# A fused linear-attention and MLP kernel: the first tile of x loaded in two halves on two queues, and the head's loads and steps in a new order

## The chip, the cores and the metric

The kernel runs on one NeuronCore of a Trainium2 chip. The metric is device time in microseconds, from the median of several executions. Instructions run on TensorE (PE; its weight loads are listed as PEld), VectorE (DVE), ScalarE (ACT), GpSimd (POOL) and SyncE (SP, which here only issues transfers). ScalarE issues some transfers too. In the profile a queue's issue of a transfer stands as SPq or ACTq.

## The reference

With S = 2048 tokens, width D = 640, 32 heads of 20 and a hidden width of 1728, it computes, in bf16:

```python
xn = layernorm(x)                              # over the last axis
qkv = (xn @ wqkv).reshape(B, S, 3, 32, 20).transpose(2, 0, 3, 1, 4)
q, k, v = qkv[0], qkv[1], qkv[2]
phi = lambda t: where(t > 0, t + 1, exp(t)) + 1e-6
kv  = einsum("bhsd,bhse->bhde", phi(k), v)
z   = einsum("bhsd->bhd", phi(k))
num = einsum("bhqd,bhde->bhqe", phi(q), kv)
den = einsum("bhqd,bhd->bhq", phi(q), z)[..., None] + 1e-6
s   = (num / den).transpose(0, 2, 1, 3).reshape(B, S, D) @ wo
g   = silu(relu(xn @ w1) @ w2)
out = x + s * g
```

## The kernel before, in words

The tokens are 16 tiles of 128 rows, tile t being x rows 128 t to 128 t + 127. The kernel's body records operations (engine, what is read, what is written) with a small scheduler, and the scheduler then works out every wait. The order in which operations are recorded is a text, PROGRAM (line 346), of short words that a player (line 1572) looks up. Up to the bar "|" the text is the head: there every engine keeps the text's order. Behind the bar TensorE and SP still keep it, while VectorE, ScalarE and GpSimd take, of the steps that are ready, those that are due first by the planner's costs (lines 44 to 83 for compute, 147 to 166 for transfers; lags, line 205, are two delays that the planner adds to the transfer line once it has passed a given time).

The words that matter here:

- lxN loads tile N of x (160 KB) on SP's queue, line 562; axN does so on ScalarE's queue. lkAB loads rows 128 A to 128 B of the key weight, 160 KB for each 128 rows, line 586. lwN loads a block of w1 (320 KB), line 582.
- baN and bbN take VectorE's statistics over the first and the second half of tile N (line 637), agN combines them (line 641). For tiles 0 and 3 the mean of the first half comes from VectorE (mhN, line 679) and of the second half from ScalarE (maN, line 685); for tiles 1 and 2 ScalarE sums the whole row. ceN subtracts the mean (lines 695 and 699; for tile 0 in two parts).
- trN transposes the centred tile with five TensorE products against an identity (line 706), cdN and caN copy the result to SBUF on VectorE or ScalarE (lines 716 and 718). kTAB multiplies tile T with key weight rows A to B (line 733); each such row block is two products of 320 columns. In the head only tiles 0 to 3 go this way.
- sqN squares a centred tile on ScalarE for its variance. SN and NN are statistics and norm of the other tiles (lines 637 to 673); each norm is followed by a DMA transpose on SP (line 722). Tiles 0 to 7 are transposed so in the head, in the order 1, 4, 5, 7, 6, 0, 2, 3.
- keN and krN are the exponential and the relu of the key product (line 743), FN their sum (lines 759 and 761). PN is a block of relu(x w1) over the first four tiles (line 823, with lw blocks 2 and 5 for P4, P5, P10 and P11). KTN is the key product of a later tile, from the DMA transposes (line 733).
- pfN and the products at the start (fill, line 604) are idle products: TensorE multiplies constants, 128 columns for each unit of the count, in products of up to 512 columns. The result is never read.

Behind the bar come Strassen-like units of seven products (line 1164 for 512-column ones, line 991 for 320-column ones) with operand sums on VectorE (line 936); the first such unit over tiles 0 to 7 needs all eight DMA transposes. The rest of the program, some 170 us, is made of such units and their evacuation, and the output of the last tiles.

The order around the change, in the head before, is this on each queue. SP: x0, x2, key weight 0 to 2, x3, key weight 2 to 4, x4, x5, key weight 4 to 5, x7, w1 block 2, x6, w1 blocks 5, 3 and 0, then the eight DMA transposes. ScalarE: x1, then the means of tiles 0, 1 and 2. VectorE: first half of tile 0's statistics, half mean, centring of tiles 0 and 1, first copy, second half of the statistics, centring of tile 2, two more copies. TensorE: 32 units of idle products, transposition of tile 0, three units of idle products, transposition of tile 1, key products of tile 0, transposition of tile 2, and so on.

Of the kernel before, what the change touches and what calls it, by code (L numbers as in the profile page):

```python
# [4 lines left out]
ALU = mybir.AluOpType  # L5
# [90 lines left out]
class Sched:  # L96
# [43 lines left out]

    def _record(self, E, kind, fns, R, W, extra, sem=None):
        o = _Op()
        o.E, o.kind, o.fns, o.n = E, kind, fns, len(self.recs)
        o.sem, o.need = sem if isinstance(sem, tuple) else (sem, 16)
        o.deps = set(self._hazards(R, W)) | set(extra)
        o.byt = 0
        if kind == "dma":
            seen = _Seen()
            fns[0](seen)
            name, a, _k = seen.call  # L150
            o.turn = "transpose" in name
# [35 lines left out]
    def place(self):  # L187
# [7 lines left out]
        t = sum(o.occ for o in queue["PE"]) + 10.0  # L195
# [15 lines left out]
        while left:  # L211
# [23 lines left out]
            est, E, c = best  # L235
# [115 lines left out]
SH0_1 F2 lx8 lq SH0_2 F3 lw6 wb KT7 KT6 xb wa SQ S8 xa n8 H110 n12 F6 H14 a0.s1 rb n11 F7  # L351
SM F4 SH0_3 xc T0 SH0_4 n13 H15 SK a0.s5 a0.s6 a0.s2 n9 H111 a0.s7 p1.s1 a0.s3 p1.s5 a0.s4 SH1 p1.s6 n10 n14 n15
y0 p1.s2 m0.s1 m0.s5 p1.s3 m0.s6 p1.s7 m0.s2 y4 y3 m0.s7 p1.s4 m0.s3 Kb8 m0.s4 a1.s5 a1.s1 F5 y2 Ka12 p0.s1 y1 p0.s5 a1.s6
a1.s2 p0.s6 a1.s7 a1.s3 y7 Ka8 a1.s4 p0.s2 a2.s5 a2.s1 y8 p0.s3 p0.s7 a2.s6 y5 y6 hh0 Ka11 T1 a2.s7 p0.s4 a2.s2 a2.s4 a2.s3
# [3 lines left out]
b2.s4 m1.s1 GT1 b2.s3 GT2 m1.s5 b3.s1 m1.s6 m1.s2 b3.s5 b3.s6 m1.s7 m1.s3 b3.s2 ZS b3.s7 b3.s3 m1.s4 c1 b5.s1 b3.s4 b5.s5 b4.s5 b5.s6  # L358
b4.s1 b5.s2 b5.s7 sl b4.s6 b5.s3 zc w2b b5.s4 b4.s7 b4.s3 g0.s1 g0.s5 b4.s4 g0.s6 b4.s2 GT3 w2c dn hh1 w2d GT4 wo g0.s3
GS1 g1.s1 do0 g1.s5 g0.s2 g1.s6 g0.s7 rc0 g1.s7 do1 g1.s2 dv0 g1.s3 g1.s4 wv1 uSa0 uT1 g0.s4 uT3 wv0 uT2 uSb0 u0.s1 u0.s5  # L360
kv1 do2 kv0 rc1 W5 u0.s6 uT4 W4 u0.s2 W1 u0.s7 uSa1 W3 u0.s3 uSa2 uSb2 W0 u1.s1 u0.s4 W2 uSb1 u1.s5 u1.s6 u2.s5
u2.s1 u1.s2 u1.s7 oT u2.s6 u1.s3 u1.s4 oS0 u2.s2 xre o0.s1 u2.s7 uSa4 o0.s5 o0.s6 u2.s3 do3 u2.s4 o0.s7 o0.s2 oS1 o0.s3 uSa3 u4.s1
# [8 lines left out]
def bass_recurrent_scan__linear_attn_block__dense_activation_relu__prompt_kernel(  # L371
# [14 lines left out]
    P = 128  # L386
# [6 lines left out]
    HN = D // 2  # L393
# [5 lines left out]
    x2 = A_x[0]  # L399
# [45 lines left out]
    xin = reg7[:, :].rearrange("p (t n) -> p t n", t=XR)  # L445
# [4 lines left out]
    def eks(t):  # L450
        return t % 4 if t < 8 else t % 3
# [33 lines left out]
    F0 = 6 * D  # L485
# [71 lines left out]
    def xs(t):  # L557
        return t if t < XR else (t - 4) % XR

    def x_load(t, n=1, E="SP", extra=()):  # L560
        sl = xs(t)
        dma(E, lambda eng: eng.dma_start(xin[:, sl:sl + n, :],
                                         x2[P * t:P * (t + n), :].rearrange("(t p) n -> p t n", p=P)),
            W=[("xin", sl + i) for i in range(n)], extra=extra)
# [39 lines left out]
    def fill(n):  # L604
        sc.group("PE", [(lambda eng, w=w: eng.matmul(ps[7][:, 0:w], lhsT=wide[:, 0:P], rhs=wide[:, 0:w], start=True, stop=True))
                        for w in [4 * P] * (n // 4) + [P * (n % 4)] * (n % 4 > 0)], W=[("ps", 7)])
# [28 lines left out]
    def bn(t, a):  # L635
        xv = xin[:, xs(t), :]
        sc.op("DVE", lambda eng: eng.bn_stats(stats[:, t, a, :], xv[:, HN * a:HN * (a + 1)]),  # L637
              R=[("xin", xs(t))], W=[("stats", t, a)])
# [44 lines left out]
    def mean_act(t, lo):  # L683
        junk = ek[:, eks(t), 0, 0:D - lo]
        sc.op("ACT", lambda eng: eng.activation(out=junk, in_=xin[:, xs(t), lo:D], func=ACTF.Copy, scale=1.0 / D,
                                                accum_out=msum[:, t, 1:2]),
              R=[("xin", xs(t))], W=[("msum", t, 1), ("ek_e", eks(t))])
        sc.allow_unread.add(("ek_e", eks(t)))

    def centre(t):  # L690
        split = ((0, P * TS), (P * TS, D)) if t == 0 else ((0, D),)
        for part, (c0, c1) in enumerate(split):
            key = ("xn", t, 0) if t == 0 and part == 0 else ("xn", t)
            if t in (1, 2):
                sc.op("DVE", lambda eng, c0=c0, c1=c1: eng.tensor_scalar(
                    out=xn[:, t, c0:c1], in0=xin[:, t, c0:c1], scalar1=msum[:, t, 1:2], scalar2=None,
                    op0=ALU.subtract), R=[("xin", t), ("msum", t, 1)], W=[key])
            else:
                sc.op("DVE", lambda eng, c0=c0, c1=c1: eng.tensor_scalar(
                    out=xn[:, t, c0:c1], in0=xin[:, t, c0:c1], scalar1=msum[:, t, 0:1], scalar2=msum[:, t, 1:2],  # L700
                    op0=ALU.subtract, op1=ALU.subtract), R=[("xin", t), ("msum", t, 0), ("msum", t, 1)], W=[key])
# [1280 lines left out]
```

## Time and profile before

| what | value |
|---|---|
| runs, device time | 202.53, 202.60 and 204.0 us; median 202.60 |
| the profiled execution | 202.56 us |
| its span, first to last instruction | 201.3 us |
| TensorE busy | 197.2 us, 98% of the span |
| VectorE, ScalarE, GpSimd busy | 173.2, 132.5, 37.7 us |
| transfers | 30.43 MB, 151 GB/s on the mean |

The span is shorter than the execution by what lies around the first and the last instruction. A row of the timeline has start, length, engine, line, operation, what is written and read, and at its end how long the engine stood idle before it and what released it. The rows of the chain of waits have start, length and what held the program's end in that stretch. TensorE's products are pipelined and their ends are modelled, so two products in a row overlap by the latency; the distance of two starts is the true cost of one.

### The profile page before, as it was taken

Reading aid. Unit: us, or ns where it says so; the run is one execution under the profiler, and the core shown is the slowest. Engines: PE = TensorE matmul, PEld = TensorE weight load, DVE = VectorE, ACT = ScalarE, POOL = GpSimd, SP = SyncE. Lnnn points to the kernel's source line nnn. Section 1 sums busy time; section 2 is a strip of 40 time slices with the busy share of each in tenths; the row PEclk is TensorE's granted clock in tenths of the full one; section 3 lists DMA queues with packets and bytes.
Section 4 is the critical chain, followed back from the end, with each engine's and each line's share of the span. In section 5 each row is a group of like instructions: output and inputs, shape, how many; then the busy total and the mean of one; then the engine's idle time right before and its main releaser. Section 6 shows DMA issues by size and latency. Waiting matters only on the chain.

```text
span 201.3 us, 3641 instructions
## 1 busy us (share of the span) xinstructions
PE 197.2 (98%) x1312; PEld 120.1 (60%) x1312; DVE 173.2 (86%) x407; ACT 132.5 (66%) x280; POOL 37.7 (19%) x66
## 2 busy tenths in 40 slices
PE   8899999999999999999999999999999999999995
PEld 2656534554564554545454777777777777777773
DVE  5998799999999989999568998999867699866565
ACT  6798958998999998868832514363545355536533
POOL 3584003143345646422000000000000000000000
PEclk9999999999999999999999999999999999999999
DMA  5999695345466798854304985975952711011113
GB/s 179 335 259 95 150 351 144 70 98 109 108 145 134 150 256 174 171 99 67 113 17 118 270 264 184 295 212 148 355 185 72 258 65 36 33 67 65 36 65 98
DMA packets 38455, 30.43 MB, mean 151 GB/s; under 512 B 13733, under 2 KB 38437, under 8 KB 38437
## 3 DMA queue, kind: packets, MB, share of 16 engines
q1 hardware_dynamic: 32853, 23.62, 41.8%
q0 software_dynamic: 4624, 5.57, 14.3%
q10 hardware_dynamic: 960, 1.02, 1.7%
q8 instruction: 10, 0.16, 0.4%
q14 instruction: 8, 0.07, 0.1%
HBM read 15.81 MB, written 5.24 MB: 105 GB/s over the span
## 4 chain that ended last, share of the span: by engine, by line
PE 90%; DVE 4%; DMA 2%; ACT 1%; issue 1%; DVEq 0%
PE psT L991 43%; PE psT L1164 32%; PE psT L733 6%; PE psT L1494 2%; PE psT L823 2%; DMA reg<-reg 1%; ACT regE L743 1%; PE psT L1838 1%; DMA reg<-in_A_x_dram 1%; PE psT L841 1%; PE psT L1629 1%; PE psT L1603 1%; DVE stats L637 1%; DVE regX L936 1%; PE psT L895 1%
## 5 line engine op out<-in xcount | busy, mean ns | idle before, releaser
L1164 PE MATMUL psT<-reg 128*128 128x512 bf16 (+2 forms) x166 | 45.0, 370 | 0.0
L991 PE MATMUL psT<-reg,regH 128*128 128x320 bf16 (+1 forms) x224 | 35.0, 299 | 0.0
L991 PE MATMUL psT<-reg 128*128 128x320 bf16 (+1 forms) x178 | 28.4, 299 | 0.0
L991 PEld LDWEIGHTS psT<-reg,regH 128*128 128x128 bf16 (+1 forms) x224 | 21.9, 98 | 8.5
L1164 PEld LDWEIGHTS psT<-reg 128*128 128x128 bf16 (+1 forms) x166 | 15.9, 98 | 16.9 <-DVE regH L1217 0.6
L863 POOL DMA_DIRECT2D regH<-reg x16 | 18.6, 1188 | 20.9 <-DMA regH<-reg 9.4
L991 PEld LDWEIGHTS psT<-reg 128*128 128x128 f16 (+1 forms) x178 | 17.3, 98 | 7.4 <-DVE regE L899 0.4
L936 DVE TENSOR_TENSOR reg<-reg 128x1024 f16<-128x1024 bf16 (+11 forms) x30 | 19.0, 646 | 2.2 <-PE psT L991 1.8
L998 ACT ACTIVATE reg<-psT 128x320 f32<-128x320 f32 (+1 forms) x24 | 10.5, 436 | 15.8 <-PE psT L991 14.8
L1214 ACT ACTIVATE regH<-psT 128x512 bf16<-128x512 f32 (+1 forms) x24 | 14.6, 612 | 5.8 <-PE psT L1164 5.3
L1665 ACT ACTIVATE wv_sb<-psT 128x320 bf16<-128x320 f32 (+2 forms) x23 | 9.6, 424 | 11.4 <-PE psT L991 11.0
L991 PE MATMUL psT<-reg,pqT 128*128 128x320 bf16 (+1 forms) x84 | 15.8, 299 | 0.0
L936 DVE TENSOR_TENSOR psT<-psT,reg 128x320 f32<-128x320 f32 (+1 forms) x21 | 11.4, 543 | 2.8 <-PE psT L991 2.8
L637 DVE BATCH_NORM_STATS2 stats<-reg 128x6 f32<-128x320 bf16 x28 | 12.3, 480 | 1.4 <-DMA reg<-in_A_x_dram 1.1
L1853 ACT ACTIVATE reg<-psT 128x640 bf16<-128x640 f32 (+1 forms) x14 | 8.0, 570 | 7.5 <-PE psT L991 7.5
L733 PE MATMUL psT<-reg 128*128 128x320 bf16 x80 | 12.3, 299 | 0.0
L936 DVE TENSOR_TENSOR reg<-psT,reg 128x320 bf16<-128x320 f32 (+1 forms) x16 | 7.8, 489 | 5.1 <-PE psT L991 5.1
L1171 ACT ACTIVATE psT<-psT 128x512 f32<-128x512 f32 (+1 forms) x18 | 10.6, 594 | 1.8 <-PE psT L1164 1.7
L800 ACT ACTIVATE regE<-psT 128x512 bf16<-128x512 f32 x16 | 9.5, 603 | 2.6 <-PE psT L1164 2.5
L998 ACT ACTIVATE psT<-psT 128x320 f32<-128x320 f32 x17 | 7.2, 425 | 5.6 <-PE psT L991 5.5
L936 DVE TENSOR_TENSOR reg<-reg,wv_sb 128x640 bf16<-128x640 bf16 (+1 forms) x15 | 6.8, 456 | 4.3 <-ACT reg L1853 3.5
L733 PEld LDWEIGHTS psT<-reg 128*128 128x128 bf16 x80 | 7.7, 98 | 4.5 <-issue 0.4
(174 smaller groups left out, 400.0 us busy)
## 6 DMA issues: line engine op xcount, KB each, us to landing
regH<-reg POOLq DMA_DIRECT2D x16, 320.0 KB, 3.8
reg<-in_B_w_dram SPq DMA_DIRECT2D x12, 320.0 KB, 4.9
scr<-rden SPq DMA_DIRECT2D x4, 640.0 KB, 7.0
reg<-in_A_x_dram SPq DMA_DIRECT2D x4, 640.0 KB, 6.1
out_dram<-reg SPq DMA_DIRECT2D x14, 160.0 KB, 1.8
regE<-scr SPq DMA_DIRECT2D x3, 640.0 KB, 6.1
reg<-in_A_x_dram SPq DMA_DIRECT2D x4, 320.0 KB, 4.8
reg<-in_A_x_dram SPq DMA_DIRECT2D x7, 160.0 KB, 4.3
```

Of the source, the lines that this page charges most:

```text
L637: sc.op("DVE", lambda eng: eng.bn_stats(stats[:, t, a, :], xv[:, HN * a:HN * (a + 1)]), R=[("xin", xs(t))], W=[("stats", t, a)])
L733: fns.append(lambda eng, a=a, k=k, lhs=lhs: eng.matmul(ps[bk[a]][:, 0:HN], lhsT=lhs, rhs=wk[:, k, HN * a:HN * (a + 1)], start=(k == 0), st ...
L800: exps.append(sc.op("ACT", lambda eng: eng.activation(out=e_, in_=src, func=ACTF.Exp), R=[key], W=[("er_e", es)]))
L863: dma("POOL", lambda eng: eng.dma_start(zacc[a], src, **kw), R=[key] + after, W=[("zacc", a)], chain=zchain[a])
L936: sc.op("DVE", lambda eng: eng.tensor_tensor(out=out, in0=in0, in1=in1, op=op), R=R, W=W, extra=extra)
L991: sc.group("PE", [(lambda eng, k=k, lhs=lhs, rhs=rhs: eng.matmul(ps[b][:, 0:HN], lhsT=lhs, rhs=rhs, start=(start and k == 0), stop=(k == n ...
L998: sc.op("ACT", lambda eng: eng.activation(out=dst, in_=ps[b][:, 0:HN], func=ACTF.Copy), R=[("ps", b)], W=[dkey], extra=extra)
L1164: sc.group("PE", [(lambda eng, k=k, lhs=lhs, rhs=rhs: eng.matmul(ps[b][:, 0:nn], lhsT=lhs if tile is None else rhs, rhs=rhs if tile is Non ...
L1171: sc.op("ACT", lambda eng: eng.activation(out=dst[:, 0:nn], in_=ps[b][:, 0:nn], func=ACTF.Copy), R=[("ps", b)], W=[dkey], extra=extra)
L1214: sc.op("ACT", lambda eng: eng.activation(out=dst, in_=ps[b], func=ACTF.Relu), R=[("ps", b)], W=[("hT", j, f)], extra=ex)
L1665: sc.op("ACT", lambda eng, lo=lo, hi=hi: eng.activation(out=g[:, lo:hi], in_=src[:, lo - HN * n:hi - HN * n], func=ACTF.Silu), R=[key, ("s ...
L1853: sc.op("ACT", lambda eng: eng.activation(out=o_[:, 0:n].rearrange("p (a n) -> p a n", a=2) if n == D else o_[:, 0:n], in_=src, func=ACTF. ...
```

## The change

Tile 0 is loaded as two transfers of 320 columns (80 KB each), the first half by SP, the second by ScalarE's queue, with a key of its own for the second half, which the readers of those columns get as a dependency. Tile 2 is loaded by ScalarE's queue, behind tile 1. The key weight is loaded in pieces of 160 KB, and the first two stand right behind x0 on SP. The opening idle products shrink from 32 units to 29 (seven products of 512 columns and one of 128). The planner's costs get the new transfers and another time for the first of its two delays. The text is new: in the head the second half of tile 0's statistics and its aggregate come ahead of tile 1's centring and the first copy, one copy goes from ScalarE to VectorE, w1 block 5 is loaded ahead of x6, and block P11 is computed ahead of P4. Behind the bar, neighbouring words change places. The core of the diff:

```diff
+            if names[1] == "in_A_x_dram" and size < 1e5:
+                lag, o.occ = -0.4, 0.1 if E == "ACT" else 0.5
...
-        lags = [(4.1, 0.6), (18.2, 1.2)]
+        lags = [(5.6, 0.6), (18.2, 1.2)]
...
-lx0 lx2 ax1 ba0 mh0 ma0 lk02 lx3 lk24 ce0 lx4 ma1 ce1 lx5 lk45 lx7 lw2 tr0 pf3 cd0 lx6 bb0 ma2 sq1
-ce2 cd1 ma3 tr1 k001 lw5 cd2 k012 ba3 lw3 ca3 mh3 ag0 ce3 S4 tr2 k102 S5 ca4 k023 k123 k134 ca5 k201
-lw0 N1 tr3 N4 sq2 k213 S7 ca6 k035 ca7 k145 N5 ke0 k235 S6 bb3 N7 ag3 k301 k312 kr0 ke1 kr1 F1
-N6 k325 ke2 P4 N0 kr2 P11 P5 F0 ke3 P10 KT5 kr3 KT4 N2 N3 |
+lx0 ax1 ba0 ax2 ma0 mh0 lk12 ce0 lk01 lx3 bb0 ma1 lk23 lk34 ce1 lx4 lx5 lk45 ma2 ag0 lw2 tr0 pf3 lx7
+cd0 sq1 cd1 ma3 ce2 tr1 k001 lw5 cd2 k012 lx6 ba3 cd3 mh3 ce3 S4 tr2 k102 ca4 lw3 k023 k123 lw0 k201
+S5 N1 ca5 N4 sq2 tr3 k134 k213 S7 k035 k145 ca6 ca7 N5 S6 N7 k235 bb3 ke0 ag3 k301 k312 kr0 ke1
+kr1 N6 F1 k325 P11 ke2 P4 N0 kr2 F0 P5 ke3 P10 KT5 kr3 KT4 N2 N3 |
...
     def x_load(t, n=1, E="SP", extra=()):
         sl = xs(t)
+        if t == 0:
+            for a, (Eh, key) in enumerate((("SP", ("xin", 0)), ("ACT", ("xin", 0, 1)))):
+                dma(Eh, lambda eng, a=a: eng.dma_start(xin[:, 0, HN * a:HN * (a + 1)], x2[0:P, HN * a:HN * (a + 1)]), W=[key])
+            return
...
-    fill(32)
+    fill(29)
```

More of the change, by code (lines that the diff above doesn't have):

```diff
@@ L346 @@
 PROGRAM = """
-lx0 lx2 ax1 ba0 mh0 ma0 lk02 lx3 lk24 ce0 lx4 ma1 ce1 lx5 lk45 lx7 lw2 tr0 pf3 cd0 lx6 bb0 ma2 sq1
-ce2 cd1 ma3 tr1 k001 lw5 cd2 k012 ba3 lw3 ca3 mh3 ag0 ce3 S4 tr2 k102 S5 ca4 k023 k123 k134 ca5 k201
-lw0 N1 tr3 N4 sq2 k213 S7 ca6 k035 ca7 k145 N5 ke0 k235 S6 bb3 N7 ag3 k301 k312 kr0 ke1 kr1 F1
-N6 k325 ke2 P4 N0 kr2 P11 P5 F0 ke3 P10 KT5 kr3 KT4 N2 N3 |
-SH0_1 F2 lx8 lq SH0_2 F3 lw6 wb KT7 KT6 xb wa SQ S8 xa n8 H110 n12 F6 H14 a0.s1 rb n11 F7
-SM F4 SH0_3 xc T0 SH0_4 n13 H15 SK a0.s5 a0.s6 a0.s2 n9 H111 a0.s7 p1.s1 a0.s3 p1.s5 a0.s4 SH1 p1.s6 n10 n14 n15
+lx0 ax1 ba0 ax2 ma0 mh0 lk12 ce0 lk01 lx3 bb0 ma1 lk23 lk34 ce1 lx4 lx5 lk45 ma2 ag0 lw2 tr0 pf3 lx7
+cd0 sq1 cd1 ma3 ce2 tr1 k001 lw5 cd2 k012 lx6 ba3 cd3 mh3 ce3 S4 tr2 k102 ca4 lw3 k023 k123 lw0 k201
+S5 N1 ca5 N4 sq2 tr3 k134 k213 S7 k035 k145 ca6 ca7 N5 S6 N7 k235 bb3 ke0 ag3 k301 k312 kr0 ke1
+kr1 N6 F1 k325 P11 ke2 P4 N0 kr2 F0 P5 ke3 P10 KT5 kr3 KT4 N2 N3 |
+lx8 SH0_1 lq SH0_2 lw6 F3 F2 wb KT7 KT6 xb wa SQ S8 xa n8 H110 n12 F6 H14 rb SM n11 F7
+a0.s1 F4 SH0_3 xc T0 SH0_4 n13 H15 SK a0.s5 a0.s6 a0.s2 n9 H111 a0.s7 p1.s1 a0.s3 p1.s5 a0.s4 SH1 p1.s6 n10 n14 n15
 y0 p1.s2 m0.s1 m0.s5 p1.s3 m0.s6 p1.s7 m0.s2 y4 y3 m0.s7 p1.s4 m0.s3 Kb8 m0.s4 a1.s5 a1.s1 F5 y2 Ka12 p0.s1 y1 p0.s5 a1.s6
-a1.s2 p0.s6 a1.s7 a1.s3 y7 Ka8 a1.s4 p0.s2 a2.s5 a2.s1 y8 p0.s3 p0.s7 a2.s6 y5 y6 hh0 Ka11 T1 a2.s7 p0.s4 a2.s2 a2.s4 a2.s3
+a1.s2 p0.s6 a1.s7 a1.s3 y7 Ka8 a1.s4 p0.s2 a2.s5 a2.s1 T1 y8 p0.s3 p0.s7 a2.s6 y5 y6 hh0 Ka11 a2.s7 p0.s4 a2.s2 a2.s4 a2.s3
 k1.s1 k1.s5 b0.s1 Kb12 b0.s5 y12 k1.s6 b0.s6 b0.s2 k1.s7 k1.s2 b0.s7 k1.s3 k1.s4 Kb15 b0.s4 q0.s1 b0.s3 y13 q0.s5 b1.s1 q0.s6 b1.s5 q0.s2
@@ L357 @@
 y15 k2.s2 y10 a3.s7 q1.s5 q1.s1 a3.s3 w2a a3.s4 q1.s6 GS0 q1.s2 b2.s5 zm b2.s1 q1.s7 q1.s3 b2.s6 b2.s2 q1.s4 b2.s7 SH2 zs c0
[L358 to L362, printed above, removed]
+b2.s4 m1.s1 GT1 b2.s3 m1.s5 b3.s1 GT2 m1.s6 m1.s2 b3.s5 b3.s6 m1.s7 m1.s3 ZS b3.s2 b3.s7 b3.s3 m1.s4 c1 b5.s1 b3.s4 b5.s5 b4.s5 b5.s6
+b4.s1 b5.s2 b5.s7 sl b4.s6 b5.s3 zc w2b b5.s4 b4.s7 b4.s3 g0.s1 g0.s5 b4.s4 g0.s6 b4.s2 GT3 w2c dn hh1 w2d g0.s3 GT4 wo
+GS1 g1.s1 g1.s5 g0.s2 g1.s6 g0.s7 do0 rc0 g1.s7 do1 g1.s2 dv0 g1.s3 g1.s4 wv1 uSa0 uT1 g0.s4 uT3 wv0 uSb0 uT2 u0.s1 u0.s5
+kv1 do2 kv0 rc1 W5 u0.s6 uT4 W4 u0.s2 W1 u0.s7 uSa1 W3 u0.s3 uSa2 uSb2 W0 u0.s4 u1.s1 W2 uSb1 u1.s5 u1.s6 u2.s5
+u2.s1 u1.s2 u1.s7 oT u2.s6 u1.s3 u1.s4 oS0 u2.s2 xre o0.s1 u2.s7 uSa4 o0.s5 o0.s6 u2.s3 u2.s4 o0.s7 o0.s2 oS1 o0.s3 uSa3 u4.s1 do3
 uSb3 dv1 uSb4 u4.s5 u4.s6 u4.s2 o0.s4 u4.s7 o1.s5 o1.s1 u4.s3 u4.s4 uSa6 rc2 o1.s6 u3.s5 oS2 u3.s1 o1.s2 o1.s7 rc3 dv2 o1.s3 u3.s6
-uSb6 o1.s4 u3.s2 o2.s1 oS3 u3.s7 uSa5 o2.s5 o2.s6 u3.s3 u3.s4 o2.s2 o2.s3 o2.s7 oS4 u5.s1 u5.s5 o2.s4 u5.s6 o3.s1 u5.s2 o3.s5 uSb5 o3.s6
-u5.s7 u5.s3 o3.s2 o3.s7 o3.s3 u5.s4 dv3 o3.s4 o4.s5 e3 o4.s1 u6.s1 u6.s5 o4.s6 u6.s6 uSa7 o4.s2 o4.s7 o4.s3 oS6 u6.s7 o4.s4 u6.s3 o5.s1
-oS5 o5.s5 u6.s4 o6.s5 o5.s6 u6.s2 o6.s1 o5.s2 o5.s7 o5.s3 e0 uSb7 o5.s4 o6.s6 u7.s5 u7.s1 o6.s7 o6.s2 o6.s3 u7.s6 u7.s2 f0 o6.s4 u7.s7
+uSb6 o1.s4 u3.s2 o2.s1 oS3 u3.s7 uSa5 o2.s5 o2.s6 u3.s3 u3.s4 o2.s2 o2.s7 o2.s3 oS4 u5.s1 u5.s5 o2.s4 u5.s6 o3.s1 u5.s2 o3.s5 uSb5 o3.s6
+u5.s7 u5.s3 o3.s2 o3.s3 o3.s7 u5.s4 dv3 o3.s4 o4.s5 e3 o4.s1 u6.s1 u6.s5 o4.s6 u6.s6 uSa7 o4.s2 o4.s7 o4.s3 oS6 u6.s7 o4.s4 u6.s3 o5.s1
+oS5 o5.s5 u6.s4 o6.s5 o5.s6 u6.s2 o6.s1 o5.s2 o5.s7 o5.s3 e0 uSb7 o5.s4 o6.s6 u7.s5 u7.s1 o6.s7 o6.s2 u7.s6 o6.s3 o6.s4 u7.s2 f0 u7.s7
 u7.s3 f3 e1 f1 u7.s4 l0 l1
@@ L637, in bn @@
         sc.op("DVE", lambda eng: eng.bn_stats(stats[:, t, a, :], xv[:, HN * a:HN * (a + 1)]),
-              R=[("xin", xs(t))], W=[("stats", t, a)])
+              R=[("xin", xs(t))] + ([("xin", 0, 1)] if t == 0 and a == 1 else []), W=[("stats", t, a)])
     def aggr(t):
@@ L674, in LN_norm @@
             out=xn[:, t, :], in0=xin[:, xs(t), :], scalar1=mean, scalar2=rsy[:, t:t + 1],
-            op0=ALU.subtract, op1=ALU.mult), R=[("xin", xs(t)), key, ("rsy", t)], W=[("xn", t)]))
+            op0=ALU.subtract, op1=ALU.mult), R=[("xin", xs(t)), key, ("rsy", t)] + ([("xin", 0, 1)] if t == 0 else []), W=[("xn", t)]))
         xnT_dma(t)
@@ L686, in mean_act @@
                                                 accum_out=msum[:, t, 1:2]),
-              R=[("xin", xs(t))], W=[("msum", t, 1), ("ek_e", eks(t))])
+              R=[("xin", 0, 1) if t == 0 else ("xin", xs(t))], W=[("msum", t, 1), ("ek_e", eks(t))])
         sc.allow_unread.add(("ek_e", eks(t)))
@@ L700, in centre @@
                     out=xn[:, t, c0:c1], in0=xin[:, t, c0:c1], scalar1=msum[:, t, 0:1], scalar2=msum[:, t, 1:2],
-                    op0=ALU.subtract, op1=ALU.subtract), R=[("xin", t), ("msum", t, 0), ("msum", t, 1)], W=[key])
+                    op0=ALU.subtract, op1=ALU.subtract),
+                    R=[("xin", t), ("msum", t, 0), ("msum", t, 1)] + ([("xin", 0, 1)] if t == 0 else []), W=[key])
     def transposes(t, b):
```

## The prediction

> **What bounds the kernel now.** I read the page's head first, then busy time by stage (the windows view), TensorE's waits, the chain that ended last, and last the first 30 us instruction by instruction, with the transfers.
>
> The page: span, then busy time of the engines.
>
> ```profile
> span 201.3 us, 3641 instructions
> PE 197.2 (98%) x1312; PEld 120.1 (60%) x1312; DVE 173.2 (86%) x407; ACT 132.5 (66%) x280; POOL 37.7 (19%) x66
> ```
>
> The windows view: stretch, length, busy time (instructions) of PE, PEld, DVE, ACT and POOL, granted clock, DMA share, GB/s.
>
> ```profile
> 0.83:4.20 3.37, 3.37 (x8) 1.01 (x8) 1.95 (x6) 2.50 (x5) 1.36 (x6) 1.00 0.64 192
> 4.20:6.04 1.84, 1.07 (x12) 0.69 (x12) 1.84 (x8) 1.67 (x6) 0.08 (x1) 1.00 1.00 324
> ...
> 22.00:28.60 6.60, 6.38 (x30) 2.52 (x29) 5.88 (x14) 4.96 (x10) 0.00 (x0) 1.00 0.89 261
> 28.60:110.80 82.20, 82.20 (x482) 41.51 (x483) 76.31 (x184) 67.39 (x141) 26.92 (x33) 1.00 0.59 128
> 110.80:196.00 85.20, 85.20 (x648) 61.77 (x647) 69.73 (x149) 40.12 (x89) 0.00 (x0) 1.00 0.49 154
> ```
>
> From 28.6 to 196 us TensorE has no idle time at all. So a gain can only come from how early its unbroken stream passes 28.6, and whatever is gained before and lost again by then is nothing. The profiled execution took 202.56 us, 1.26 beyond its span and 0.04 below the median of the three runs (202.60). The runs shown reach from 202.53 to 204.0.
>
> The chain that ended last, in order of time (start, length, what), for the head:
>
> ```profile
> 0.79 2.34 DMA reg<-in_A_x_dram
> ...
> 3.15 0.51 DVE stats L637
> ...
> 3.68 0.23 DVE msum L679
> ...
> 3.93 0.64 DVE reg L699 x2
> 4.57 0.30 DVE reg L695
> 4.87 0.20 DVE regX L716
> 5.07 0.40 DVE stats L637
> ...
> 6.04 0.70 PE psT L733 x4
> ...
> 8.93 3.26 PE psT L733 x24
> ```
>
> The chain says: x0 lands at 3.13, VectorE takes half a tile's statistics, the half mean and the centring, and copies the transposed tile; the first key product starts at 6.04. TensorE's waits put that start down to VectorE:
>
> ```profile
> PE psT L733 <- DVE regX L716: 0.6, 1, 0.6
> PE psT L1164 <- DVE psT L936: 0.2, 1, 0.2
> ```
>
> But the copy that this product needs was done at 5.07 (4.87 + 0.20). The late one is a transfer. The timeline of the head, and the transfers' own rows (the DMA view on a sliver of time; last column us from issue to landing), for the key weight lk02 and the w1 block lw5:
>
> ```profile
> 0.83 3.38 PE L605 MATMUL psT<-const-bfloat16-1.0 128*128 128x512 bf16 x8 [0.83 <-PEq L1967]
> 0.96 0.39 ACTq L562 DMA_DIRECT2D reg<-in_A_x_dram  x1
> 1.71 0.43 SPq L586 DMA_DIRECT2D reg<-in_A_wqkv_dram  x1
> 3.53 0.19 ACT L685 ACTIVATION_READ_ACCUMULATOR regE<-reg 128x1 f32 x1
> 3.77 0.44 PE L605 MATMUL psT<-const-bfloat16-1.0 128*128 128x512 bf16 x1
> 4.33 0.11 PEld L706 LDWEIGHTS psT<-ident,reg 128*128 128x128 bf16 x2 [0.84 <-DVE reg L699]
> 6.19 0.43 SPq L582 DMA_DIRECT2D reg<-in_B_w_dram  x1
> 6.34 0.49 DVE L637 BATCH_NORM_STATS2 stats<-reg 128x6 f32<-128x320 bf16 x1
> 7.70 0.49 DVE L637 BATCH_NORM_STATS2 stats<-reg 128x6 f32<-128x320 bf16 x1
> 11.76 0.49 DVE L637 BATCH_NORM_STATS2 stats<-reg 128x6 f32<-128x320 bf16 x1
> 12.03 0.38 PE L823 MATMUL psT<-regX,reg 128*128 128x512 bf16 x1
> ```
> ```profile
> reg<-in_A_wqkv_dram SPq DMA_DIRECT2D x1, 320.0 KB, 4.2
> ```
> ```profile
> reg<-in_B_w_dram SPq DMA_DIRECT2D x1, 320.0 KB, 5.9
> ```
>
> lk02 was issued at 1.71 and landed at 5.9, 0.1 before the first key product. So two chains of nearly one length meet at 6.04, and only a change that shortens both moves it.
>
> The second bound lies further back: the eight DMA transposes of x, which the first Strassen unit needs all of.
>
> ```profile
> 10.17 12.16 SPq L722 DMA_TRANSPOSE reg<-reg  x8
> ```
> ```profile
> 17.07 2.61 SPq L722 DMA_TRANSPOSE reg<-reg  x1
> ```
> ```profile
> 21.05 1.28 SPq L722 DMA_TRANSPOSE reg<-reg  x1
> ```
> ```profile
> reg<-reg SPq DMA_TRANSPOSE x1, 2.6
> ```
> ```profile
> q8 instruction: 1, 0.02, 97.6%
> ```
> ```profile
> 18.00:18.50 0.50, 0.50 (x6) 0.37 (x4) 0.50 (x2) 0.50 (x1) 0.00 (x0) 1.00 0.00 0
> ```
> ```profile
> 23.72 0.43 DVE L936 TENSOR_TENSOR regH<-reg 128x512 f16<-128x512 bf16 x1 [0.45 <-DMA reg<-reg]
> ```
> ```profile
> 28.58 0.39 PE L1164 MATMUL psT<-regX,reg 128*128 128x512 f16 x1 [0.17 <-DVE psT L936]
> ```
>
> SP issues them without a pause for 12.16 us; the usual one holds it 1.28, the sixth 2.61 (from 17.07). In that hole no DMA moved a byte (18.0 to 18.5: 0 GB/s), and an instruction fetch of 0.02 MB runs at 17.0 to 17.1. The last is issued at 21.05 and lands 2.6 later, at 23.65; VectorE starts the operand sums at 23.72, and TensorE waits for VectorE at 28.58. An earlier TensorE alone gains nothing past this point.
>
> **The change part by part.**
>
> x0 in halves. SP issues half a at 0.79, ScalarE half b at about 0.96 (where its x1 is now). A half has half of the data time; by the next tile 160 KB cost 0.4 us (lk02 ended at 5.9, x3 let VectorE start at 6.34), so half a lands 0.2 sooner, at 2.93. Bounds: 0 sooner (3.13), and 0.4 (2.73). Half b, issued 0.17 later, lands at 3.13 to 3.15, as the whole did. The first statistics start 0.2 sooner, and the half mean ends 0.78 after half a (3.15 to 3.93): 3.73. ScalarE's mean of half b ends 0.57 after it starts, as now (3.72). So centring starts at about 3.78 and not 3.93: 0.15 gained, ScalarE the later of the two.
>
> VectorE's order. The second statistics half (0.40) now stands ahead of tile 1's centring, with an aggregate (I estimate 0.13 from the spacing of short VectorE steps such as 0.20 and 0.23). The first copy ends at 3.78 + 0.64 + 0.40 + 0.30 + 0.13 + 0.20 = 5.45, against 5.07 now: 0.4 later, and nevertheless before the 6.04 at which the product starts.
>
> Key weight right behind x0. lk02 (320 KB) becomes two of 160 KB, second and third on SP; x2 leaves SP for ScalarE's queue. In issue order x0, lk12, x1, lk01 are 640 KB, against 800 KB to the end of lk02 now; x2, issued at about the same time, may interleave. So lk01 lands between 5.5 (5.9 less 0.4) and 5.9; below 4.0 (its issue at 1.7 + x0's 2.34) it can't be. I take 5.5. First key product: 5.55, 0.49 gained; at the other end 0.1.
>
> Idle products. Seven of 512 and one of 128 instead of eight of 512. The first seven of today's start 0.42 apart ((3.77 - 0.83) / 7), so the new ones end at 0.83 + 2.94 + 0.11 = 3.88. The transposition's weights come at 4.33 now (0.40 after centring starts), then at 4.18, so they aren't in the way. What the products buy is the step of TensorE from 0.42 to 0.216 per 512 columns (24 products of 320 in 3.26 us are 0.136 each, which is the fast rate), and that came during the last one: it took 0.44 with its latency, where the group's mean is 0.57 (the group's row: line, engine, operation, busy us, mean ns):
>
> ```profile
> L605 PE MATMUL psT<-const-bfloat16-1.0 128*128 128x512 bf16 (+1 forms) x9 | 3.7, 573 | 0.8 <-PEq L1967 0.8
> ```
>
> I cost the cut at nothing, because the step began no later than 4.2 with the transpositions already near. If that cover is gone, each key product of 320 costs 0.264 and not 0.136. The granted clock reads 1.00 throughout, so no column shows it.
> [...] The trace has the step 2.9 to 3.4 us after the first product, so it decides neither way.
>
> The rest of the head. From the first key product to the first w1 product TensorE needs 5.99 us (6.04 to 12.03) and is dense, so it would come at 11.54. That product is now P11, which needs lw5: landed at 12.1 (6.19 + 5.9) with x6 ahead of it; x6 moves behind it, 160 KB or 0.4 less, so 11.7. TensorE waits 0.2, and 0.28 of the gain is left. x6 then lands where lw5 did, 12.1, and its statistics (11.76 now) start 0.35 late; its transpose is the fifth, so I cost this at nothing: the queue of transposes covers it, and 0.35 at most if SP ran dry. x7 moves behind lw2, with room likewise. SP issues 15 transfers instead of 14 ahead of the transposes, 0.43 to 0.47 more; its last one already waits for room in the queue and the first transpose waits for its norm, so nothing. x3 and x4 have the same bytes ahead as now (960 and 1440 KB), so VectorE's steps at 6.34 and 7.70 don't move. A copy goes from ScalarE to VectorE (0.20 by the chain's) just ahead of 7.70, where VectorE waits for x4, and an aggregate has left that place.
>
> The transposes, therefore. Their first start follows x4 and x5 through the norms and stays at 10.17. Only the hole at 17.07 can move. If it belongs to TensorE's instruction fetch, it comes 0.28 sooner, as TensorE does; then the last lands at 23.37, and TensorE passes 28.58 at 28.30. That is my forecast: 202.56 - 0.28 = 202.28.
>
> The order after the head. TensorE's order changes in a few neighbouring pairs only, with equal work. VectorE's waiting steps are placed anew by the planner; one more or less ahead of the sum at 28.5 is 0.3 to 0.4 us either way. I take 0.
>
> **The rivals.**
>
> A: the transposes don't move (202.6). For: the first is bound by x4, and 12.16 us of issue follow. Against: the hole has a neighbour that moves with TensorE. Then everything gained is waited away before 28.58, and the time is 202.56.
> [...] The 0 GB/s beside the fetch speaks against it and doesn't prove the opposite.
>
> B: the fetch falls between two transposes and the hole closes (1.3 us: 2.61 - 1.28). Then TensorE binds: 0.49 is kept, the 0.22 idle of 22 to 28.6 (6.60 - 6.38) goes too, up to twice that as ends are modelled: 201.7.
>
> C, slower: TensorE's fast rate comes later, as the idle products end earlier. Place: the key products from 5.55. Price 0.13 each. It decides when the 0.49 and the 0.22 of idle are eaten, at 6 products. One more stretch of 3.2 us (to about 7.2) is some 5 products: 202.6. Two (to 10.4) are 18: +2.3 - 0.7, 204.2. I put it at 203.3.
>
> D: the change doesn't do what it says; half b lands as the whole, lk01 at 5.9, and 0.1 at most is gained: 202.5.
>
> **How the numbers follow.** Forecast 202.3 with chance 0.35; A 0.28; B 0.10; C 0.17; D 0.10. The range is 201.7 (B) to 203.3 (C's middle); it leaves out the upper half of C and a little below B. About 1% (2 us) is what a measurement can tell here from no change, so nearly every case is "same". Faster by over 1% would need the start, the idle and the whole hole: 0.02. Slower by over 1% needs C with over two stretches: 0.04. Same 0.94.
>
> **What would show it.** The first key product at 5.5 to 5.6 (right), at 5.9 or more (D). Key products 0.136 apart from the first (C wrong). The sixth transpose's hole sooner by as much as TensorE is (right), in its place (A), gone (B). The last transpose landing at 23.4, and TensorE dense from 28.3. Wrong altogether would be a stall after 28.6 that the new order brings, or x4 landing at another time than 7.7, which moves every transpose with it.

## The result, and the profile after

The kernel after takes 204.19 us (median of 10 executions, 203.25 to 205.05), the kernel before beside it 202.73 us (202.14 to 204.0): a ratio of 1.0069, 95% interval 1.0046 to 1.0092. The change costs 0.7%, where 0.3 us of gain was forecast. The profiled execution took 204.16 us. Its page, span and busy time:

```profile
span 202.8 us, 3628 instructions
PE 197.9 (98%) x1301; PEld 121.3 (60%) x1312; DVE 172.8 (85%) x408; ACT 132.4 (65%) x279; POOL 36.8 (18%) x66
```

Eleven products have no record in this trace (1301 of 1312), so a start can be missing from a row. The windows view (stretch, length, busy time of PE, PEld, DVE, ACT, POOL, granted clock, DMA share, GB/s):

```profile
4.20:6.39 2.19, 1.04 (x7) 0.41 (x7) 1.01 (x5) 1.31 (x3) 0.00 (x0) 1.00 0.99 354
6.39:14.10 7.71, 7.71 (x55) 5.68 (x57) 7.54 (x26) 5.84 (x15) 5.29 (x13) 1.00 1.14 283
...
24.00:30.20 6.20, 6.20 (x29) 2.76 (x29) 5.94 (x14) 4.82 (x9) 0.00 (x0) 1.00 1.06 341
...
112.20:197.40 85.20, 85.20 (x647) 61.64 (x647) 69.45 (x148) 40.09 (x89) 0.00 (x0) 1.00 0.49 152
```

TensorE idles half of 4.20 to 6.39 and is dense from there. It isn't stopped between 24 and 30 us any more, so nothing behind the head takes the loss back. Its first key product starts at 6.89, where 5.55 was forecast and 6.04 stood. The chain that ended last, in order of time, for the head:

```profile
1.40 3.66 DMA reg<-in_A_x_dram
5.06 0.02 issue
5.08 0.84 ACT regE L691 x2
5.92 0.02 issue
5.94 0.39 DVE reg L701
...
14.25 0.81 PE psT L830 x3
```

The transfer at its root is x1, not x0 or the key weight: issued at 1.40 behind x0's second half, landed at 5.06. ScalarE sums it, VectorE centres it, and TensorE waits for that before tile 1's transposition, which stands ahead of all key products in its order (first of its waits):

```profile
PE psT L713 <- DVE reg L701: 1.1, 1, 1.1
```

The transfers of the same moment in the DMA view, first after, then x1's in the kernel before (last column: us from issue to landing):

```profile
reg<-in_A_wqkv_dram SPq DMA_DIRECT2D x1, 160.0 KB, 3.4
reg<-in_A_x_dram ACTq DMA_DIRECT2D x1, 160.0 KB, 3.7
reg<-in_A_x_dram ACTq DMA_DIRECT2D x1, 80.0 KB, 2.1
```
```profile
reg<-in_A_x_dram ACTq DMA_DIRECT2D x1, 160.0 KB, 2.6
```

x1 was issued at 0.96 and took 2.6 us; now it is issued 0.44 later and takes 3.7, beside the key weight. The second loss is in TensorE's timeline:

```profile
4.13 0.79 PE L713 MATMUL psT<-ident,reg 128*128 128x128 bf16 x5
4.71 0.53 PE L611 MATMUL psT<-const-bfloat16-1.0 128*128 128x384 bf16 x1
6.39 0.72 PE L713 MATMUL psT<-ident,reg 128*128 128x128 bf16 x5 [1.15 <-DVE reg L701]
6.89 1.27 PE L740 MATMUL psT<-reg,regX 128*128 128x320 bf16 x4
7.96 0.74 PE L713 MATMUL psT<-ident,reg 128*128 128x128 bf16 x5
8.49 1.89 PE L740 MATMUL psT<-reg,regX 128*128 128x320 bf16 x10
```

Four key products took 0.70 before and take 1.27 here. Their starts are 0.267 apart up to 9.0 and 0.136 from 9.27 on: the fast rate, which before began at about 4.0, begins five microseconds later. The page's clock row reads 9 (90% or more) in every slice all the same. Transposes and the passage into the dense part, each from the timeline:

```profile
10.99 11.28 SPq L729 DMA_TRANSPOSE reg<-reg  x8
```
```profile
17.64 2.00 SPq L729 DMA_TRANSPOSE reg<-reg  x1
```
```profile
25.94 0.38 PE L1171 MATMUL psT<-reg 128*128 128x512 bf16 x1
```
```profile
30.04 0.38 PE L1171 MATMUL psT<-regX,reg 128*128 128x512 f16 x1
```

SP is through with issuing its last transpose when it was before (10.99 + 11.28 = 22.27; before 10.17 + 12.16 = 22.33). TensorE comes to its first unit behind the bar 2.00 us later (25.94; this product started at 23.94 before), and to the one that closed the wait of before at 30.04 instead of 28.58: 1.46 later, since two short stops of TensorE that before had between these products are gone. The span is 1.5 longer.

### The profile page after: what moved, and what is told of

Same layout as the page of the kernel before. It is cut to its first block, busy times and chain, and to the rows that moved or that the text cites. A ratio compares the mean times of both kernels' runs of the same rounds, so it can differ in the third digit from the quotient of the medians.

```text
span 202.8 us, 3628 instructions
## 1 busy us (share of the span) xinstructions
PE 197.9 (98%) x1301; PEld 121.3 (60%) x1312; DVE 172.8 (85%) x408; ACT 132.4 (65%) x279; POOL 36.8 (18%) x66
## 4 chain that ended last, share of the span: by engine, by line
PE 87%; ACT 6%; DVE 3%; DMA 2%; POOL 1%; issue 1%; DVEq 0%
PE psT L998 42%; PE psT L1171 29%; PE psT L740 5%; PE psT L830 4%; PE psT L1501 2%; DMA reg<-in_A_x_dram 2%; PE psT L1845 1%; PE psT L848 1%; ACT regE L1300 1%; DVE stats L643 1%; ACT regH L1221 1%; PE psT L1636 1%; ACT regE L750 1%; PE psT L1610 1%; ACT regE L1487 1%
## 5 line engine op out<-in xcount | busy, mean ns | idle before, releaser
L1171 PE MATMUL psT<-reg 128*128 128x512 bf16 (+2 forms) x159 | 43.1, 370 | 0.2
L740 PE MATMUL psT<-reg 128*128 128x320 bf16 x80 | 12.3, 299 | 0.0
L740 PEld LDWEIGHTS psT<-reg 128*128 128x128 bf16 x80 | 7.7, 98 | 4.5 <-issue 0.4
L998 PEld LDWEIGHTS psT<-reg,pqT 128*128 128x128 bf16 (+1 forms) x84 | 8.1, 98 | 3.3 <-DVE reg L943 0.2
```

Of the source, the lines that this page charges most:

```text
L740: fns.append(lambda eng, a=a, k=k, lhs=lhs: eng.matmul(ps[bk[a]][:, 0:HN], lhsT=lhs, rhs=wk[:, k, HN * a:HN * (a + 1)], start=(k == 0), st ...
L998: sc.group("PE", [(lambda eng, k=k, lhs=lhs, rhs=rhs: eng.matmul(ps[b][:, 0:HN], lhsT=lhs, rhs=rhs, start=(start and k == 0), stop=(k == n ...
L1171: sc.group("PE", [(lambda eng, k=k, lhs=lhs, rhs=rhs: eng.matmul(ps[b][:, 0:nn], lhsT=lhs if tile is None else rhs, rhs=rhs if tile is Non ...
```

## The experiments

Theory one, "late x1": x1's place is the loss. Theory two, "idle run": 29 units are too few to bring the fast rate in time. Theory three, "pause": TensorE's wait for x1 keeps the fast rate away. A rival: the order behind the head. Unless said otherwise a run has 12 timed executions beside 29 to 36 of the kernel before; these had medians of 202.56, 202.43 and 202.46 us in the three groups of runs. Kernels whose name begins with b are made from the kernel before and have its lines (L706 and L733 for L713 and L740); the others have after's. Code is cut to what matters, lines at their ends too.

**a_fill32**: after with 32 units.

```diff
-    fill(29)
+    fill(32)
```


> The changed kernel with 32 units of idle products again instead of 29; all else as changed. In the changed kernel the stretch from tile 1's transposition (6.39) to the first w1 product (14.03) takes 7.64 us where 15 transpositions at 0.056 and 40 key products at 0.136 make 6.28, so 1.36 us are lost to the slow rate. Theory 'idle run' (29 units end too early, so the fast rate comes a stretch late): the transpositions and all key products run at the fast rate, first w1 product at about 12.7, time 202.8 to 203.0. Theory 'pause' (x1 lands late, TensorE pauses before tile 1's transposition, and that pause keeps or makes it slow): nothing changes, 204.2.

203.59 us (202.81 to 204.83), ratio 1.0055 [1.0031, 1.008]; five of 12 above 204. So the three units account for less than half of the loss.

**b_fill29** and **b_fill29b**: the kernel before with 29 units, twice.

```diff
-    fill(32)
+    fill(29)
```


> The kernel before with 29 units of idle products instead of 32; all else as before. Theory 'idle run': key products from 6.04 on come 0.267 apart until about 9, some 1.4 us lost, of which the 0.2 to 0.5 us of later waits take a part: 203.5 to 203.9. Theory 'pause': x1 is as early as before, so the fast rate comes in time: 202.7, no change.

> The kernel before with 29 units for 32, once more, since the first time its executions fell into two groups (7 of 12 at 201.93 to 202.80, 5 at 203.22 to 204.63). Theory 'three units fewer make the fast rate come late in part of the executions': again 4 to 6 of 12 above 203.1, median 202.6 to 203.2. Theory 'no effect': at most 2 of 12 above 203.1, median within 0.2 us of before.

202.72 and 202.53 us, ratios 1.0008 [0.9979, 1.0037] and 1.0018 [0.9989, 1.0048]. The medians hardly move, but 10 of 24 executions lie above 203.1, against 8 of the kernel before's 96 beside them. The first profiled one, 204.05 us, has x0 late, a gap ahead of tile 0's transposition, and slow key products:

```profile
4.58 0.79 PE L706 MATMUL psT<-ident,reg 128*128 128x128 bf16 x5 [0.50 <-DVE reg L699]
...
6.21 1.22 PE L733 MATMUL psT<-reg,regX 128*128 128x320 bf16 x4
```

The second, 202.08 us, has the fast rate from about 3.5. So fewer units make long executions likelier, not certain; that the long ones are those with the late rate rests on these two traces.

**a_x1sp** and **a_x0whole**: x1 early by SP's queue, and x0 whole again; the planner places the rest anew.

```diff
-lx0 ax1 ba0 ax2 ma0 mh0 lk12 ce0 lk01
+lx0 lx1 ba0 ax2 ma0 mh0 lk12 ce0 lk01
```
```diff
-        if t == 0:
+        if t < 0:
...
```


> The changed kernel with x1 issued by SP right behind the first half of x0, ahead of the key weight, instead of by ScalarE's queue; 29 units of idle products. x1 should land before 3.8 instead of at 5.06, the first key product should come at about 5.6 instead of 6.89. Theory 'idle run': the fast rate is still late, so 1.0 to 1.4 us are still lost: 203.2 to 203.5. Theory 'pause': both losses go: 202.3 to 202.7.

> The changed kernel with x0 loaded whole by SP, so that x1 is the first transfer on ScalarE's queue (0.96 instead of 1.40); 29 units of idle products, all else as changed. x1 should land at about 3.6 to 4.2. Theory 'the halving made x1 late': first key product at 5.6 to 5.8; with 'idle run' still 203.2 to 203.5, with 'pause' 202.4 to 202.7. If instead the key weight ahead of x1 is to blame, x1 still lands at about 5 and the time stays at 204.2.

204.55 us (6 executions; 1.0085 [1.0056, 1.0115]) and 203.29 us (1.0032 [1.0014, 1.005]). Both traces have the fast rate by 4.9, and a_x0whole's first key product starts at 5.76, ahead of before's. They lose it at the sum that TensorE waits for behind the head. VectorE of a_x0whole, timeline:

```profile
27.88 0.43 DVE L943 TENSOR_TENSOR pqT<-reg 128x512 f16<-128x512 bf16 x1 [0.68 <-DMA reg<-in_A_wqkv_dram]
28.23 0.69 DVE L943 TENSOR_TENSOR psT<-psT,wv_sb 128x512 f32<-128x512 f32 x1
```

The planner had put an operand sum of the query weight ahead of TensorE's sum, and that weight was not there yet. In a_x1sp the same wait is 1.23 us. These two runs therefore say little on x1. In the next ones the kernel after is planned as it is, and only what is emitted changes, so the orders of VectorE, ScalarE and GpSimd stay its own.

**p_x0whole32**, **p_x0whole29**: x0 whole on SP, x1 first on ScalarE's queue, with 32 and 29 units. **p_x1sp32**, **p_x1sp29**: x0 in halves, x1 on SP's queue behind the first. Each edit acts on the list of operations in its final order:

```diff
+    x0, x1 = [[o for o in seq if o.n in sc.tag[k]][0] for k in ("x0a", "x1")]
+    seq.remove(x1)
+    x1.E = "SP"
+    seq.insert(seq.index(x0) + 1, x1)
...
+    a, b = sc.tag["x0a"][0], sc.tag["x0b"][0]
+    sc.recs[a].fns = sc.tag["whole"]
+    seq.remove(sc.recs[b])
```


> As p_x0whole29 but with 32 units at the start: of the change only the key weight ahead, the queues of x1 to x7 and the order picked anew are left. Theory 'x1 and idle products are the whole loss': one mode, 202.1 to 202.5, so 0.0 to 0.4 below before (first key product 5.76 against 6.04). Theory 'the new order costs too': 203.0 or more, as in the earlier run with x0 whole (203.29).

> The kernel after with the whole of x0 again on SyncE's queue and so x1 first on ScalarE's; 29 units kept, and the order of every engine kept as in the kernel after (in the earlier run with x0 whole the order of VectorE had changed with it). x1 lands near 3.7 us, no pause. Theory 'pause' or 'x1 late': the late rate goes with the pause, one mode, median 202.2 to 202.6, at most 1 of 12 above 203.2. Theory 'idle run': 29 units alone give what the kernel before with 29 units had, 4 to 6 of 12 executions 1.5 us above the others, median 202.6 to 203.2.

> The kernel after with x1 on SyncE's queue right behind x0's first half, ahead of the key weight, and 32 units; orders of the compute engines kept. x1 lands near 3.8 us, the second half of the key weight near 5.7, first key product 6.25. Theory 'x1 late': with x1 early and 32 units the loss shrinks to what the first key product is later (0.2 us against before): 202.5 to 203.0, one mode. Theory 'halves or queues cost by themselves': stays above 203.3.

> The kernel after, its orders and its 29 units kept, with only x1's load moved to SyncE's queue behind x0's first half. Theory 'x1 late is the loss': as with 32 units, 202.7 to 203.1, at most 3 of 12 above 204. Theory 'three units fewer are half of the loss by themselves': a third or more of the executions above 204, median 203.3 to 203.8.

| x1 | 29 units | 32 units |
|---|---|---|
| behind x0's second half (after, a_fill32) | 204.19 | 203.59 |
| on SP's queue behind the first half | 203.10 | 202.89 |
| first on ScalarE's queue, x0 whole | 202.53 | 202.42 |

p_x0whole32 is level with the kernel before (1.0005 [0.9978, 1.0031]), and p_x0whole29 within 0.1 us (1.0004 [0.998, 1.0029]). They keep after's order, the key weight ahead and x2 on ScalarE's queue. Together these cost nothing that shows, but the interval reaches from 0.4 us of gain to 0.6 of loss, so a gain as small as the forecast 0.3 could not be told from none. With 29 units one of 12 executions lies above 203.1, where the theory of the idle run expected 4 to 6: the cut that made long executions likelier in the kernel before did not do so here, and why stays open. p_x0whole32's key products start 0.15 ahead of before's, at the slow rate until 6.6 in this execution of 202.39 us:

```profile
5.39 0.71 PE L713 MATMUL psT<-ident,reg 128*128 128x128 bf16 x5
5.89 1.07 PE L740 MATMUL psT<-reg,regX 128*128 128x320 bf16 x4
```

p_x1sp32 and p_x1sp29 stand at 1.0029 each ([1.0003, 1.0055] and [1.0008, 1.005]). With x1 on SP's queue the second piece of the key weight is the late one (p_x1sp32):

```profile
6.30 0.70 PE L740 MATMUL psT<-reg,regX 128*128 128x320 bf16 x4 [0.73 <-DMA reg<-in_A_wqkv_dram]
```

p_x1sp29 came out as the theory of the late x1 expected (203.10 at the edge of 202.7 to 203.1, none above 204), though half of its executions are above 203.1. The profiled one, its longest (203.93 us), shows the rate in time and another late transfer, a w1 block:

```profile
13.36 1.89 PE L830 MATMUL psT<-regX,reg 128*128 128x512 bf16 x8 [1.18 <-DMA reg<-in_B_w_dram]
```

**b_halves**: the kernel before with x0 in halves and nothing else (the readers of the second half wait for it, as in after).

```diff
+        sl = xs(t); [dma(Eh, lambda eng, a=a: eng.dma_start(xin[:, 0, HN * a:HN * (a + 1)], x2[0:P, HN * a:HN * (a + 1)]), W=[key]) for a, (Eh, key) in enumerate((("SP", ("xin", 0)), ("ACT", ("xin", 0, 1)))) if t == 0]
-        dma(E, lambda eng: eng.dma_start(xin[:, sl:sl + n, :],
+        t and dma(E, lambda eng: eng.dma_start(xin[:, sl:sl + n, :],
...
```


> The kernel before with one part of the change alone: x0 in two halves, the second on ScalarE's queue ahead of x1, all orders and the 32 units as before. Theory 'x1 is late because it stands behind x0's second half': x1 is issued near 1.4 us and lands at 4.0 to 5.0 in place of 3.54, TensorE pauses 0.3 to 1.2 us, and the time rises by 0.3 to 1.2 us, with more executions above 204 than before's 1 in 20. Theory 'x1 is late because the key weight runs beside it': x1 lands by 4.1, and the time stays within 0.3 us of before, since the first key product waits for the key weight until 5.9 anyway.

203.32 us (202.11 to 204.97), ratio 1.0048 [1.0023, 1.0074]: this part alone costs 0.86 us at the median. Its profiled execution, however, was the fastest. Two more executions were profiled, and one more each of after and a_fill32.

> A second look at the kernel before with x0 in halves: the first profiled execution took 202.11 us (x1 landed at 4.15), 11 of 12 others 202.99 or more, and none of those was seen in a trace. Theory 'x1 late': an execution near 203.3 shows x1 landing at 4.6 or later and the first key product at 6.5 or later. Theory 'late rate': it shows x1 by 4.2 and TensorE's first key products at 0.267 us instead of 0.134.

> A third look, for the same question, with the same expectations: x1's landing at 4.6 or later against key products at 0.267 us.

> A second look at the kernel after. Theory 'x1 late': x1 lands between 4.8 and 5.2 again, first key product 6.6 to 7.0. Theory 'pause and idle run': key products at 0.267 us until about 9 if the time is above 204, at 0.134 us from the start if it is near 203.4.

> A second look at after with 32 units. Both: x1 at 4.8 to 5.2. If the time is above 204: key products at 0.267 us until about 9, which would show that the late rate comes with 32 units too when x1 is late; if it is below 203.6: at 0.134 us from the first, as in the first look.

They took 202.88, 204.21, 203.11 and 204.57 us. The rows of b_halves_3 (x1's sum on ScalarE, then TensorE) and of a_fill32_2:

```profile
4.75 0.74 ACT L685 ACTIVATE regE<-reg 128x640 bf16<-128x640 bf16 x1 [1.00 <-DMA reg<-in_A_x_dram]
```
```profile
6.05 0.72 PE L706 MATMUL psT<-ident,reg 128*128 128x128 bf16 x5 [0.68 <-DVE reg L695]
6.56 1.27 PE L733 MATMUL psT<-reg,regX 128*128 128x320 bf16 x4
```
```profile
6.76 0.71 PE L713 MATMUL psT<-ident,reg 128*128 128x128 bf16 x5 [1.50 <-DVE reg L701]
7.26 1.27 PE L740 MATMUL psT<-reg,regX 128*128 128x320 bf16 x4
```

In b_halves_2 x1's sum starts at 4.57 and four key products take 0.71, as before; in after_2 it starts at 5.05 and they take 0.71. So x1 is late by another amount each time, and the late rate comes with 32 units too once x1 is late. That an execution shows one or the other, as the expectations had it, was wrong: b_halves_3 has both.

**p_pause32** and **p_pausef32**: a_fill32 with TensorE kept busy while x1 is on its way, by 23 units in place of 3, and by three float32 products of 256 columns.

```diff
     def fill(n):
+        m = {29: 32, 3: 23}[n]
```
```diff
+        w4 = nc.const_aps.tensor(1.0, (P, 2 * P), f32)
...
+        [lambda eng: eng.matmul(ps[7][0:P, 0:2 * P], lhsT=w4[:, 0:P], rhs=w4[:, 0:2 * P], start=True, stop=True)] * 3
```


> The kernel after with 32 units of idle products at the start instead of 29 and 23 instead of 3 between x0's and x1's transposes (1.3 us more at 0.056 us each at the fast rate), so that TensorE is busy while x1 is on its way; orders of all engines kept. Theory 'pause' (a gap of 1.4 us between x0's and x1's transposes keeps the fast rate away in part of the executions): the executions above 204 that the kernel after with 32 units had (5 of 12) go, at most 1 of 12 is left, median 202.9 to 203.2. Theory 'idle run' (only the length of the first run counts): the mixture stays, 4 to 6 of 12 above 204, median 203.4 to 203.8. Both: x1's landing near 5.0 us and the first key product near 6.6 are untouched.

> As the run in which the pause was filled with 23 units, but with three float32 products of 256 columns in place of the six bfloat16 ones between x0's and x1's transposes, so that TensorE's program grows by two instructions against after with 32 units and not by five: in the earlier run the second instruction fetch had come 1.2 us earlier, at 37.88, beside a transposition on the DMA engines, and a v product waited 0.53 us at 40.9. Theory 'pause': with that wait gone the late rate is gone as well, one mode, median 202.8 to 203.4, at most 1 of 12 above 204. Theory 'x1 late, whatever TensorE does meanwhile': 4 to 6 of 12 above 204 as with the pause open, median 203.5 to 203.9. If the products last longer than the pause, tr1 is late by that and the median rises by it.

204.11 us (203.41 to 204.52; 1.0076 [1.0053, 1.0099]) and 203.97 us (8 executions, 203.33 to 204.56; 1.0074 [1.0047, 1.0101]). p_pause32 lies above everything expected of it. p_pausef32, with four of eight above 204, comes nearest to the theory that the lateness of x1 costs the same whatever TensorE does meanwhile. The traces say more than the times. Both have the fast rate, from about 5.75. Tile 1's transposition stands right behind the idle products (p_pause32, timeline), at 6.52 and 6.58, 0.4 to 0.5 us after VectorE was through with centring that tile (6.02 and 6.16), so the filled pause is longer than x1 needs:

```profile
4.73 1.95 PE L611 MATMUL psT<-const-bfloat16-1.0 128*128 128x512 bf16 x6
6.52 0.44 PE L713 MATMUL psT<-ident,reg 128*128 128x128 bf16 x5
```

The largest single loss is behind the head (p_pausef32, timeline; 0.53 in p_pause32):

```profile
41.55 0.72 PE L740 MATMUL psT<-reg 128*128 128x320 bf16 x4 [0.62 <-DMA reg<-reg]
```

By the starts of TensorE's weight loads, counted from the program's end, 0.7 and 0.8 us of the 1.5 and 1.6 by which these two traces end behind a_fill32's (202.94 us) arise here; the rest comes in smaller steps elsewhere and is not explained. A DMA transposition landed at 40.9 and 41.5 instead of 39.3 in a_fill32. The instruction fetch that lay at 39.04 there began at 37.89 and 38.91, inside it; that the fetch did it is argued from the times alone. The kernel before has the same pairing in its head: the transpositions issued at 15.75 and 17.07, in flight at its fetch of 17.05, landed 4.5 and 4.0 us later, and the two behind them 2.6. An execution with the late rate would probably come to that product after the landing and not wait. So the times of these runs don't tell late executions from others, and that a filled pause always brings the rate in time is not shown; the two traces have it so.

The starts show where the rate changes, in the 18 executions traced: between 3.5 and 6.7 us in 14, between 9.2 and 10.2 in four, nowhere in between. For eight of them, with TensorE's wait ahead of tile 0's or tile 1's transposition (timeline):

| execution | rate changes at | wait, us | it ends at |
|---|---|---|---|
| p_pause32, 204.44 us | 5.75 | none | |
| p_x0whole32, 202.39 us | 6.63 | none | |
| a_fill32, 202.94 us | 3.53 | 1.39 | 6.29 |
| p_x1sp29, 203.93 us | 5.66 | 0.45 | 5.58 |
| b_fill29, 204.05 us | 10.2 | 0.50 | 4.58 |
| b_halves_3, 204.21 us | 9.62 | 0.68 | 6.05 |
| after, 204.16 us | 9.25 | 1.15 | 6.39 |
| a_fill32_2, 204.57 us | 9.85 | 1.50 | 6.76 |

All four late executions have such a wait ahead of the change, with half rate before and behind it; in a_fill32 it begins 1.4 us after the change and the fast rate stays (four key products in 0.71). But p_x1sp29 has the fast rate 0.08 us behind its 0.45, and after_2 went at half rate into a wait of 1.02 us that ends at 6.36 (384 columns in 0.53) and came out at the fast one (four key products in 0.71). So the length of the wait alone doesn't decide, and what does is not shown. In four executions (after_2, a_x0whole, b_halves, b_halves_2) the change falls into a pause and can't be placed closer. The late rate stands in traces with 29 units and x1 early (b_fill29) and with 32 units and x1 late (a_fill32_2, b_halves_3); whether theories two and three are one mechanism is not shown. The pause runs were to tell and, by the times, could not.

## Why the prediction was wrong, point by point

- "x0 in halves" held as a step: the first half landed at 2.81 (2.93 forecast), and centring started at 3.72 (3.78). This is all that the halves gain, and it reaches nothing; what they cost, 0.86 us alone in b_halves, stands in no term.
- "Key weight right behind x0" failed, in its last line: "First key product: 5.55". The step followed bytes up to lk01 and counted x1 among them, but never costed x1's own landing, though x1 moved behind half b and beside two pieces of the key weight, and tile 1's transposition stands ahead of the first key product. x1 landed at 5.06 in place of 3.54, and the product started at 6.89. lk01 itself landed 4.0 after its issue at 1.71, at 5.7, inside its bounds: it would have allowed 0.3 of gain. The prediction's own rule, that only a change which shortens both chains moves the start, was applied to two chains where there are three.
- "Idle products", costed at nothing, failed. The cover that was named (the step begins by 4.2) isn't the same in each execution (the traces have the change from 3.5 to 10.2). Alone the cut moves the median by 0.1 to 0.2 us, inside the intervals, and 10 of 24 executions lie 0.8 us or more above the median of the others; with x1 late it is 204.19 against 203.59.
- The price in rival C was right: 0.267 in place of 0.136 a product, at the place named. Its whole stretches of 3.2 us are shown by no run: the traces have the change between 3.5 and 6.7 us or between 9.2 and 10.2, and not why. That the 204.2 worked out in it meets the 204.19 measured is luck: it was 2.3 for half rate from 5.55 to 10.4 less 0.7 of gains, while the profiled execution has no gain, 0.85 of a later start, 1.15 of half rate up to 9.27, and 0.54 of earlier stops back. Its cause was half named (the idle products, not the wait for x1), and its chance of 0.17 and its midpoint of 203.3 were too low; the 204.2 lay outside the range.
- "The transposes, therefore" forecast a first start of 10.17; it was 10.99. x4 had landed at 7.5, but VectorE, busy without a pause from tile 1's late centring on (5.94 in place of 4.57), took its statistics at 8.55 in place of 7.70:

```profile
8.55 0.86 DVE L643 BATCH_NORM_STATS2 stats<-reg 128x6 f32<-128x320 bf16 x2
```

That the last issue ended at 22.27 all the same, against 22.33, is chance: the hole shrank from 2.61 to 2.00, and the first issue took 0.27 less. The hole came 0.57 later (17.07 to 17.64) and the fetch beside it 0.82 later (17.05 to 17.87) while TensorE was some 2.0 late, so they didn't move with TensorE as forecast. The two traces of a_fill32 show the same: the fetch lies at 19.65 and at 17.92, and TensorE is 1.6 later in the second. The hole no longer mattered, since TensorE came later than the transposes. The added transfer cost SP nothing, as forecast: the issue of its last load ahead of the transposes ended at 9.49 before (7.41 + 2.08) and at 9.53 now (7.59 + 1.94). The other loads' issues take 0.40 to 0.70; that the last one waits for room in the queue is read from its length alone.
- "The order after the head" at 0 held: TensorE is 1.46 late at 30.04 and 1.5 at the end, and p_x0whole32 has that order at before's time. It held for this order only: a_x0whole's cost 0.8 us (203.29 against p_x0whole29's 202.53).
- Where the 1.46 comes from, in the profiled execution: 0.85 from the first key product's later start (6.04 to 6.89; some 0.2 of it is the half rate in tile 1's transposition, whose starts are 0.107 apart in place of 0.056), about 1.15 from the half rate until 9.27 (2.00 at 25.94, less 0.85), less 0.54 of before's waits. Over the executions, undoing x1's place gives 1.7 us at 29 units and undoing the three units 0.6 with x1 late: the two overlap.

## What to carry to other kernels

When a transfer is split over a second queue, follow what already stood on that queue to its consumer, and not only the transfer that was meant to gain; an engine in a fixed order waits for the last of all of them (here TensorE, 1.15 us for x1). Idle work ahead of the first products must be costed with the waits that follow it, and over executions, since a gap that is harmless in one trace (a_fill32's) goes with key products at half rate up to 9.9 us in another (a_fill32_2's). And when one step is undone for an experiment, keep the planner from moving everything else.

## What was not expected of the hardware

- x1's landing was set by its last parts: in after's trace 14 of its 16 parts were in by 4.2, the last two at 4.88 and 5.06, and ScalarE starts at 5.08.
- The first half of x0 (80 KB) took 2.0 us from issue to landing in after, the whole tile at the same place 2.3 before: halving saved 0.3 us, not half.
- x1's time from issue to landing differs between the kernels. It took 2.6 to 2.8 us when it was issued at 0.96 (six traces, three of them with the key weight behind x0). Issued near 1.39 behind half b it took 2.8 to 3.3 with x2 on SP's queue just ahead (three traces of b_halves), and 3.4 to 4.0 with a piece of the key weight there (six traces). So its own place and the other queue's load both seem to go into it, but no run here moves the key weight alone. x1 on SP's queue made the key weight late instead (0.73 us of wait).
